# Forgetting attention and a spectral mix: rows 0 to 127 of each weight matrix loaded as row pairs

## The chip, the cores and the metric

The kernel runs on one core of one Trainium2 chip. The metric is the device time of one launch in microseconds. Every run is of the whole kernel, from inputs in the chip's main memory (HBM) to the output there. Engines are called as the profile calls them: PE (TensorE; PEld is its weight load), DVE (VectorE), ACT (ScalarE), POOL (GpSimd), SP (SyncE), and the 16 DMA engines.

## The reference

```python
def _attn_ref(q, k, v, f):                  # q, k, v: (8, 8, 576, 64), f: (8, 8, 576)
    scores = (1.0 / np.sqrt(D)) * np.matmul(q, k.transpose(0, 1, 3, 2))
    cum = np.cumsum(np.log(np.clip(f, 0.0001, 1.0)), axis=-1)
    scores = np.where(causal, -1000000000.0, scores + cum[:, :, :, None] - cum[:, :, None, :])
    attn = softmax(scores)
    return np.matmul(attn, v)

def _moe_ref(x, w_r, w_i, w_ch):            # x: (8, 576, 512), w_r, w_i: (64, 512, 512)
    X = np.fft.rfft(x, axis=1)
    Xr, Xi = np.real(X[:, :64]), np.imag(X[:, :64])
    Yr = np.einsum('bmd,mde->bme', Xr, w_r) - np.einsum('bmd,mde->bme', Xi, w_i)
    Yi = np.einsum('bmd,mde->bme', Xr, w_i) + np.einsum('bmd,mde->bme', Xi, w_r)
    Y[:, :64] = Yr + 1j * Yi
    u = x + np.fft.irfft(Y, n=576, axis=1)
    return u + np.maximum(u @ w_ch, 0.0)
```

Attention over 64 pairs of batch and head gives `x` (8 batches, 576 positions, 512 channels). Along the positions `x` is transformed to 64 frequencies ("modes"). Each mode m has a complex 512 by 512 matrix, `w_r[m] + i w_i[m]`, that is applied to the 8 batches' spectra. The result is transformed back, added to `x`, and goes through one more matrix, `w_ch`. All inputs are float32. The two weight arrays have 64 MiB each and are by far the most of what is read.

## The kernel before, in words

**Attention.** The 64 batch-head pairs are handled two heads at a time: 32 steps, `pairs[i] = (g, b)`, where g (0 to 3) names a group of two heads, 128 channels of `x`, and b is the batch. Group 0 comes first for all eight batches, then group 1, and so on. The loop over `i` has 34 turns; its body is written in a fixed order by hand, and every engine works through its own instructions in that order. In turn `i`, `scores(i, ..)`, `mask` and `back_v` work on step `i`, `trans(i + 1, ..)` and `scale_v(i + 1)` prepare the next, `av` and `norm` finish step `i - 1` and write its part of `x_all` (bf16), and `dft(i - 2)` computes the spectrum of the step before that. POOL's queue issues nearly all loads in program order: in turn `i` q and k of step `i + 4` (five buffers), v of step `i + 3` (four buffers), and one or two halves of a weight tile.

**The spectrum.** `dft` multiplies `x_all[:, g, b, ..]` (positions on the partitions) with the basis `bas3` (blocks sin, cos, -sin of 64 columns each; line 310) into PSUM. For groups 0 and 1 it is five matmuls (one for each block of positions) with all 128 channels as output partitions and 192 columns (line 505). One ACT copy (line 512) puts the result into `XS[:, g]`, ordered mode, block, batch. A slice of 16 columns of one mode then holds (real, imaginary) or (-imaginary, real) for 8 batches, the operand for `w_r` or `w_i`. For groups 2 and 3 the channels are split into even and odd ones, ten matmuls of 64 output partitions (line 521), and copied into `XP` (line 528): partitions 0 to 63 hold pairs of channels of group 2, 64 to 127 those of group 3.

**Weight tiles.** A tile `(u, dc)` belongs to four modes, 4u to 4u + 3, and has 1024 KB in bf16 (the load converts from float32). For `dc` 0 and 1 it holds rows 128·dc to 128·dc + 127 of both `w_r` and `w_i`, one row for each partition, so that each contiguous piece that a DMA reads is one row, 2048 B; the two arrays are two DMAs ("halves", line 156). For `dc` 2 and 3 it holds rows 256 to 511 of one of the two arrays, two neighbouring rows on each partition, so that each piece is 4096 B (line 165). The order of tiles is `wseq`: `(0,0)` to `(15,0)`, `(0,1)` to `(11,1)`, then for each u `(u,1)` if it is not yet there, `(u,2)`, `(u,3)`. There are seven buffers in `wpool`; five of the first tiles are "guests" in space that `x_all` and `yx` need only later.

**Matrix products.** `spec_mms` multiplies one tile, four modes by two parts, eight matmuls with 512 columns (line 194); the four modes go to four groups of 32 output partitions. In attention, from turn 10, `spec_early` does so for the first 28 tiles and adds the results up in `yacc`, that is `yx[:, h, 0:1024]`. After attention, the mode stage goes through u = 0 to 15 with the other tiles, adds `yacc` (line 815), and turns the outcome into `YT`; `xw` and `folds` of the batches are put between. For u = 15 `spec_cols` (line 211) takes the place of `spec_mms`. After the last weight tile the last modes are transformed back and all outputs written, the tail.

Of the kernel before, what the change touches and what calls it, by code (L numbers as in the profile page):

```python
# [10 lines left out]
F32 = mybir.dt.float32  # L11
BF16 = mybir.dt.bfloat16
# [5 lines left out]
def _strided(ap: bass.AP, free_dims, offset_elems: int = 0) -> bass.AP:  # L18
    new_ap = [list(ap.ap[0])] + [list(x) for x in free_dims]
    return bass.AP(tensor=ap.tensor, offset=ap.offset + offset_elems, ap=new_ap)  # L20
# [3 lines left out]
def kernel(  # L24
# [11 lines left out]
    nc = tc.nc  # L36
    B, H, S, Dh = q.shape
    NM = moe_w_r.shape[0]
    D = H * Dh
    assert S == 576 and Dh == 64 and D == 512 and H == 8, (B, H, S, Dh)  # L40
    assert NM == 64 and B == 8
    NSB = 5
    SBLK = [128, 128, 128, 128, 64]
# [9 lines left out]
    XROW = 24 * NM + 32  # L53
# [8 lines left out]
    const = ctx.enter_context(tc.tile_pool(name="const", bufs=1))  # L62
    wpool = ctx.enter_context(tc.tile_pool(name="wpool", bufs=NW))

    yx = const.tile([128, 8, 1280], F32, name="yx")
    x_all = const.tile([128, NEB, B, NSB, 128], BF16, name="x_all")
    XS = const.tile([128, 2, XROW], BF16, name="XS")
    XP = const.tile([128, 2, 24, NM], BF16, name="XP")
    wch = const.tile([128, NEB, D], BF16, name="wch")
    ident_bf = const.tile([128, 128], BF16, name="ident_bf")  # L70
# [5 lines left out]
    bas3 = const.tile([128, NSB, 3, NM], BF16, name="bas3")  # L76
# [21 lines left out]
    psM = actx.enter_context(tc.tile_pool(name="psM", bufs=2, space=PSUM))  # L98
# [28 lines left out]
    for u in range(NU):  # L127
# [4 lines left out]
    guests = {  # L132
        0: x_all[:, 3, :, :, :].rearrange("p b s c -> p (b s c)"),
        2: x_all[:, 2, :, :, :].rearrange("p b s c -> p (b s c)"),
        4: yx[:, 6:8, :].rearrange("p k e -> p (k e)").bitcast(BF16),
        6: yx[:, 4:6, :].rearrange("p k e -> p (k e)").bitcast(BF16),
        11: x_all[:, 3, :, :, :].rearrange("p b s c -> p (b s c)"),
    }

    def issue_w(half=None):  # L140
        n = wissued[0]
        if n >= len(wseq):
            return
        u, dc = wseq[n]
        if half != 1:
            if n in guests:
                w8 = guests[n][:, 0 : 8 * D].rearrange("p (t m e) -> p t m e", t=2, m=4)
            else:
                shape = [128, 2, 4, D] if dc < 2 else [128, 4, 2, D]
                w8 = wpool.tile(shape, BF16, tag="w8", name="w8")  # L150
            wtile[(u, dc)] = w8
        w8 = wtile[(u, dc)]
        if dc < 2:
            for t, src in enumerate((moe_w_r, moe_w_i)):
                if half in (None, t):
                    nc.gpsimd.dma_start(  # L156
                        w8[:, t, :, :],
                        src[4 * u : 4 * u + 4, dc * 128 : (dc + 1) * 128, :].rearrange("m p e -> p m e"),
                    )
        elif half != 1:  # L160
            src = (moe_w_r, moe_w_i)[dc - 2]
            step = 1 if n + 1 == len(wseq) else 4
            for j in range(0, 4, step):
                m = 4 * u + j
                nc.gpsimd.dma_start(  # L165
                    w8[:, j : j + step, :, :].rearrange("p m r e -> p m (r e)"),
                    src[m : m + step, 256:512, :].rearrange("m (p r) e -> p m (r e)", r=2),
                )
        if half != 0:
            wissued[0] += 1  # L170
# [3 lines left out]
    def issue_half():  # L174
        issue_w(whalf[0])
        whalf[0] ^= 1

    XPv = XP[:].rearrange("p r c m -> p (r c) m")

    def spec_mms(A, u, dc, first, last):  # L180
        w8 = wtile.pop((u, dc))
        for n in range(2):
            for j in range(4):
                m = 4 * u + j
                st_, sp_ = first and n == 0, last and n == 1
                if dc < 2:
                    M = 32
                    c0 = m * 24 + (8 if n == 0 else 0)
                    lhsT, rhs = XS[:, dc, c0 : c0 + 32], w8[:, n, j, :]
                else:  # L190
                    M = 32 if st_ else 16
                    c0 = 24 * n + (8 if dc == 2 else 0)
                    lhsT, rhs = XPv[:, c0 : c0 + M, m], w8[:, j, n, :]
                nc.tensor.matmul(  # L194
                    A[32 * j : 32 * j + M, :], lhsT=lhsT, rhs=rhs, start=st_, stop=sp_
                )

    def spec_cols(AT, dc, modes=range(4)):
        u = NU - 1
        w8 = wtile[(u, dc)]  # L200
        for j in modes:
            for eb in range(NEB):
                for n in range(2):
                    m = 4 * u + j
                    if dc < 2:
                        c0 = m * 24 + (8 if n == 0 else 0)
                        lhsT, rhs = w8[:, n, j, eb * 128 : (eb + 1) * 128], XS[:, dc, c0 : c0 + 16]
                    else:
                        c0 = 24 * n + (8 if dc == 2 else 0)
                        lhsT, rhs = w8[:, j, n, eb * 128 : (eb + 1) * 128], XPv[:, c0 : c0 + 16, m]  # L210
                    nc.tensor.matmul(
                        AT[:, eb, 2 * j : 2 * j + 2, :].rearrange("p c b -> p (c b)"),
                        lhsT=lhsT,
                        rhs=rhs,
                        start=(n == 0),
                        stop=(n == 1),
                    )
# [95 lines left out]
        nc.vector.tensor_copy(bas3[:, :, 2, :], Zt[:, :, :, 1])  # L313

    def setup_late():
        nc.vector.memset(XS[:, :, 24 * NM : XROW], 0.0)
        nc.vector.tensor_copy(
            perm[:].rearrange("p (b j ri) -> p b j ri", b=8, j=4),
            ident_bf[:].rearrange("p (j x ri b) -> p b j x ri", j=4, x=2, ri=2)[:, :, :, 0, :],
        )  # L320
        nc.vector.tensor_copy(rep[:], _strided(ident_bf[:, KF:128], [[0, 4], [1, KL]]))
        nc.gpsimd.dma_start(wch[:], moe_w_ch.rearrange("(eb p) e -> p eb e", p=128))
# [175 lines left out]

    def dft(i):
        g, b = pairs[i]  # L500
        if g < 2:
            pd = psM.tile([128, 3, NM], F32, tag="m", name="pd")
            for sc in range(NSB):
                ns = SBLK[sc]
                nc.tensor.matmul(
                    pd[:],
                    lhsT=x_all[:ns, g, b, sc, :],
                    rhs=bas3[:ns, sc, :, :],
                    start=(sc == 0),
                    stop=(sc == NSB - 1),  # L510
                )
            nc.scalar.copy(
                XS[:, g, 0 : 24 * NM].rearrange("p (m c b) -> p c m b", c=3, b=8)[:, :, :, b], pd[:]
            )
            return
        pd = psM.tile([128, 2, 3, NM], F32, tag="m", name="pd2")
        half = slice(64 * (g - 2), 64 * (g - 2) + 64)
        for r in range(2):
            for sc in range(NSB):
                ns = SBLK[sc]  # L520
                nc.tensor.matmul(  # L521
                    pd[half, r, :, :],
                    lhsT=x_all[:ns, g, b, sc, r:128:2],
                    rhs=bas3[:ns, sc, :, :],
                    start=(sc == 0),
                    stop=(sc == NSB - 1),
                )
        nc.scalar.copy(
            XP[half, :, :, :].rearrange("p r (c b) m -> p r c b m", c=3)[:, :, :, b, :], pd[half]
        )  # L530
# [3 lines left out]
    def spec_early(u, dc):  # L534
        if u == NU - 1:
            AT = psM.tile([128, NEB, 8, B], F32, tag="m", name="AT0")
            spec_cols(AT, dc)
            nc.vector.tensor_copy(accT[:], AT[:].rearrange("p e c b -> p e b c"))
            return
        A = psM.tile([128, D], F32, tag="m", name="A0")  # L540
        spec_mms(A, u, dc, True, True)
        if dc == 0:
            nc.scalar.copy(yacc[u // 2][:, u % 2, :], A[:])
        else:
            y = yacc[u // 2][:, u % 2, :]
            nc.vector.tensor_tensor(y, A[:], y, ALU.add)
# [5 lines left out]
    for i in range(NPAIR + 2):  # L552
# [54 lines left out]
        if i >= 2:  # L607
            dft(i - 2)
        if i == 2:
            setup_late()  # L610
# [12 lines left out]
    with ExitStack() as bctx:  # L623
# [44 lines left out]
        with ExitStack() as mctx:  # L668
# [97 lines left out]
            for u in range(NU):  # L766
# [4 lines left out]
                for dc in range(first, NEB):  # L771
# [3 lines left out]
                    if last:  # L775
# [6 lines left out]
                        else:  # L782
# [16 lines left out]
                            for h in range(2):  # L799
                                for to, frm, n in ((YLa[h], 0, 4), (YLw[h], 2, 2), (YLw[h], 0, 2)):  # L800
# [7 lines left out]
                                    )  # L808
                    else:
                        spec_mms(A, u, dc, dc == first, dc == NEB - 1)  # L810
                    issue_w()
                if last:
                    break
# [3 lines left out]
                for eb in range(NEB):  # L817
                    nc.tensor.matmul(
                        yps[:, eb, :],
                        lhsT=Yb[:, eb * 128 : (eb + 1) * 128],  # L820
                        rhs=perm[:],
                        start=True,
                        stop=True,
# [93 lines left out]
        for i in range(len(steps)):  # L917
# [11 lines left out]
            p, sb = steps[i][0]  # L929
# [54 lines left out]
```

## Time and profile before

| | |
|---|---|
| Time, median of 3 runs | 436.8 us (436.75 to 438.17) |
| Profiled execution, its own time | 436.43 us |
| Its span in the profile | 434.6 us |
| Busy: PE, DVE, ACT, POOL | 343.3, 267.9, 234.1, 145.0 us |
| Read from HBM, written to it | 163.7 MB, 9.4 MB |
| DMA packets of POOL's queue (q0) | 62800 |
| Half of a `dc` 0 or 1 tile: issue to landing | 11.1 us (`w_r`), 12.3 us (`w_i`), 27 each, 512 KB |
| A `dc` 2 or 3 tile: issue to landing | 29.5 us (16 of `w_r`), 31.7 us (15 of `w_i`), 1024 KB |

The span is the time from the profile's first to its last instruction; the difference to the execution's own time, 1.8 us, lies around it. Busy time is the time in which an engine executes, not how much of its peak it reaches. The profile counts a DMA's bytes as written, so a float32 load into bf16 moves twice that in reading. Its DMA share adds up the times of all packets over 16 engines; packets overlap, so it can be over 1.

### The profile page before, as it was taken

Reading aid. Unit: us, or ns where it says so; the run is one execution under the profiler, and the core shown is the slowest. Engines: PE = TensorE matmul, PEld = TensorE weight load, DVE = VectorE, ACT = ScalarE, POOL = GpSimd, SP = SyncE. Lnnn points to the kernel's source line nnn. Section 1 sums busy time; section 2 is a strip of 40 time slices with the busy share of each in tenths; the row PEclk is TensorE's granted clock in tenths of the full one; section 3 lists DMA queues with packets and bytes.
Section 4 is the critical chain, followed back from the end, with each engine's and each line's share of the span. In section 5 each row is a group of like instructions: output and inputs, shape, how many; then the busy total and the mean of one; then the engine's idle time right before and its main releaser. Section 6 shows DMA issues by size and latency. Waiting matters only on the chain.

```text
span 434.6 us, 10304 instructions
## 1 busy us (share of the span) xinstructions
PE 343.3 (79%) x4264; PEld 189.6 (44%) x4274; DVE 267.9 (62%) x651; ACT 234.1 (54%) x358; POOL 145.0 (33%) x215
## 2 busy tenths in 40 slices
PE   1689787798898898988896386599877498888993
PEld 1455555554555565555553142244433233334330
DVE  6677888877778778888885122222233165565794
ACT  4556777687887766656660022024322166564783
POOL 6544445444544353444213211111122202110273
PEclk9986999999999999999999579589999699999998
DMA  8999999999999999999999999999999999998498
GB/s 185 205 233 220 233 219 232 225 227 233 231 229 227 226 228 225 228 225 228 227 218 213 212 212 211 212 212 213 211 212 212 209 209 211 210 209 158 168 383 323
DMA packets 68543, 96.76 MB, mean 223 GB/s; under 512 B 3728, under 2 KB 45200, under 8 KB 68496
## 3 DMA queue, kind: packets, MB, share of 16 engines
q0 software_dynamic: 62800, 85.64, 106.3%
q1 hardware_dynamic: 5696, 10.47, 6.6%
q8 instruction: 33, 0.54, 0.4%
q14 instruction: 14, 0.11, 0.1%
HBM read 163.73 MB, written 9.44 MB: 398 GB/s over the span
## 4 chain that ended last, share of the span: by engine, by line
DMA 43%; PE 31%; DVE 18%; issue 3%; ACT 3%; POOL 1%; DVEq 0%; POOLq 0%
DMA w<-in_moe_w_r_dram 22%; DMA w<-in_moe_w_i_dram 20%; PE pav L477 5%; DVE vT L384 4%; DVE qkT L360 4%; DVE x_all L492 4%; PE A L194 4%; PE sps L432 3%; PE tv L382 3%; PE pd L521 3%; PE vp L393 2%; DMA qk<-in_k_dram 2%; PE Z L654 2%; DVE vn L372 2%; PE U L654 2%
## 5 line engine op out<-in xcount | busy, mean ns | idle before, releaser
L439 ACT ACTIVATE et<-sps 128x1024 bf16<-128x1024 f32 x96 | 96.0, 1049 | 13.9 <-PE sps L432 11.5
L477 PE MATMUL pav<-vs,et 128*128 128x65 bf16 (+1 forms) x896 | 52.1, 198 | 0.2 <-DVE vn L372 0.2
L360 DVE COPY qkT<-tp 128x640 bf16<-128x640 bf16 x64 | 48.7, 763 | 2.8 <-PE tp L355 2.8
L815 DVE TENSOR_TENSOR Yb<-A,yx 128x512 bf16<-128x512 f32 x15 | 10.4, 691 | 61.0 <-PE A L194 60.9
L477 PEld LDWEIGHTS <-et 128*128 128x128 bf16 (+1 forms) x896 | 37.2, 103 | 17.9 <-issue 13.6
L432 PE MATMUL sps<-qkT 64*128 64x512 bf16 (+4 forms) x320 | 39.8, 312 | 1.1 <-DVE qkT L360 1.1
L194 PE MATMUL A<-w,XP 128*16 128x512 bf16 (+1 forms) x240 | 21.9, 449 | 23.0 <-DMA w<-in_moe_w_i_dram 12.8
L694 PE MATMUL pxw<-wch,xT 128*128 128x512 bf16 (+1 forms) x152 | 39.0, 402 | 0.9 <-issue 0.3
L492 DVE TENSOR_TENSOR x_all<-pav,rcp 128x384 bf16<-128x384 f32 (+2 forms) x96 | 36.2, 377 | 3.3
L355 PE MATMUL tp<-ident_bf,qk 128*64 128x128 bf16 x576 | 30.3, 237 | 9.3 <-DMA qk<-in_k_dram 9.3
L384 DVE COPY vT<-tv 128x576 bf16<-128x576 bf16 x32 | 24.2, 757 | 19.8 <-PE tv L382 19.8
L165 POOL DMA_DIRECT2D w<-in_moe_w_r_dram x16 | 11.9, 743 | 71.8 <-PE A L194 50.5
L701 ACT CAST XW<-pxw 128x512 bf16<-128x512 f32 (+1 forms) x16 | 9.4, 585 | 47.3 <-PE pxw L694 47.3
L156 POOL DMA_DIRECT2D w<-in_moe_w_r_dram x27 | 20.5, 758 | 38.7 <-DMA w<-in_moe_w_i_dram 9.4
L404 ACT COPY vs<-vp 128x576 bf16<-128x576 bf16 x32 | 20.5, 640 | 21.7 <-PE vp L400 21.7
L165 POOL DMA_DIRECT2D w<-in_moe_w_i_dram x19 | 13.3, 698 | 53.3 <-PE A L194 31.6
L701 ACT CAST yx<-pxw 128x512 bf16<-128x512 f32 (+1 forms) x24 | 14.0, 585 | 31.4 <-PE pxw L694 31.4
L109 POOL DMA_DIRECT2D qk<-in_q_dram x32 | 19.5, 610 | 32.5 <-PE sps L432 6.2
L741 ACT CAST x_all<-pu 128x512 bf16<-128x512 f32 (+1 forms) x40 | 23.4, 584 | 11.2 <-PE pu L740 10.3
L491 DVE RECIPROCAL rcp<-pav 128x6 f32<-128x6 f32 (+2 forms) x96 | 16.2, 169 | 17.4 <-PE pav L477 17.3
L156 POOL DMA_DIRECT2D w<-in_moe_w_i_dram x27 | 20.3, 752 | 18.4 <-DMA w<-in_moe_w_i_dram 8.2
L109 POOL DMA_DIRECT2D qk<-in_k_dram x32 | 19.2, 601 | 19.3 <-DMA w<-in_moe_w_i_dram 5.2
(149 smaller groups left out, 677.8 us busy)
## 6 DMA issues: line engine op xcount, KB each, us to landing
w<-in_moe_w_r_dram POOLq DMA_DIRECT2D x16, 1024.0 KB, 29.5
w<-in_moe_w_i_dram POOLq DMA_DIRECT2D x15, 1024.0 KB, 31.7
w<-in_moe_w_r_dram POOLq DMA_DIRECT2D x27, 512.0 KB, 11.1
w<-in_moe_w_i_dram POOLq DMA_DIRECT2D x27, 512.0 KB, 12.3
out_dram<-o_sb SPq DMA_DIRECT2D x36, 256.0 KB, 3.2
vt<-in_v_dram POOLq DMA_DIRECT2D x29, 288.0 KB, 10.7
qk<-in_q_dram POOLq DMA_DIRECT2D x32, 144.0 KB, 10.8
qk<-in_k_dram POOLq DMA_DIRECT2D x32, 144.0 KB, 10.4
```

What stands on the lines that cost most here:

```text
L109: nc.gpsimd.dma_start(qk[64 * n : 64 * n + 64, :, :], src[b, 2 * g : 2 * g + 2, :, :].rearrange("h (p r) d -> p h (r d)", p=64),)
L156: nc.gpsimd.dma_start(w8[:, t, :, :], src[4 * u : 4 * u + 4, dc * 128 : (dc + 1) * 128, :].rearrange("m p e -> p m e"),)
L165: nc.gpsimd.dma_start(w8[:, j : j + step, :, :].rearrange("p m r e -> p m (r e)"), src[m : m + step, 256:512, :].rearrange("m (p r) e -> p ...
L194: nc.tensor.matmul(A[32 * j : 32 * j + M, :], lhsT=lhsT, rhs=rhs, start=st_, stop=sp_)
L355: nc.tensor.transpose(tp[64 * hp : 64 * hp + 64, r - r0, :, :].rearrange("p n c -> p (n c)"), qk[:, hp, r * 64 : r * 64 + 64], ident_bf[:, :],
L360: nc.vector.tensor_copy(st[i]["T"][:].rearrange("p n (c r) -> p n c r", r=9)[:, :, :, r0:r1], tp[:, 0 : r1 - r0, :, :].rearrange("p r n c ...
L384: nc.vector.tensor_copy(st[i]["vT"][:].rearrange("p (c r) -> p c r", r=9), tv[:].rearrange("p r c -> p c r"))
L432: nc.tensor.matmul(ps[:, hp, c : c + n], lhsT=KT[sl, jb * 128 : jb * 128 + 128], rhs=QT[sl, i0 : i0 + n], start=True, stop=True,)
L439: nc.scalar.activation(st[i]["et"][:, T, :, :], ps[:], ACT.Exp, scale=scale)
L477: nc.tensor.matmul(pav[:Ms, sb % 3, hp, :], lhsT=eblk(i, hp, jb, sb), rhs=rhs, start=(jb == 0), stop=(jb == sb),)
L492: nc.vector.tensor_tensor(x_all[:ns, g, b, lo:hi, :].rearrange("p s (h d) -> p s h d", h=2), pav[:ns, lo % 3 : lo % 3 + n, :, 0:Dh], _stri ...
L694: nc.tensor.matmul(pxw[rows, :], lhsT=xT[:, eb, sb * 128 : sb * 128 + Ms], rhs=wch[:, eb, :], start=(eb == 0), stop=(eb == NEB - 1),)
```

## The change

Tiles `(u, 0)`, rows 0 to 127, get another layout. The 128 rows of `w_r` become 64 pairs of neighbouring rows, 4096 B each, on partitions 0 to 63; the 128 rows of `w_i` become 64 pairs on partitions 64 to 127. A tile keeps its size and its two DMAs, which now write 64 partitions each. The spectrum of group 0 must match: partitions 0 to 63 need channel pairs as `w_r` multiplies them, partitions 64 to 127 the same pairs as `w_i` does. `dft` for g = 0 therefore makes twenty matmuls of 64 output partitions and 128 columns (even and odd channels, five blocks of positions, two halves of partitions), and two ACT copies into a new place, `x0`, which lies in `yx[:, h, 1024:1280]` for h = 2, 3, 5, 7. `XS` keeps group 1 alone. The two matmuls of a mode in `spec_mms` are now the even and the odd rows rather than `w_r` and `w_i`.

```diff
-    XS = const.tile([128, 2, XROW], BF16, name="XS")
+    XS = const.tile([128, XROW], BF16, name="XS")
...
-                    nc.gpsimd.dma_start(
-                        w8[:, t, :, :],
-                        src[4 * u : 4 * u + 4, dc * 128 : (dc + 1) * 128, :].rearrange("m p e -> p m e"),
-                    )
+                    rows = src[4 * u : 4 * u + 4, dc * 128 : (dc + 1) * 128, :]
+                    if dc == 0:
+                        nc.gpsimd.dma_start(
+                            w8[64 * t : 64 * t + 64, :, :, :].rearrange("p m r e -> p m (r e)"),
+                            rows.rearrange("m (p r) e -> p m (r e)", r=2),
+                        )
+                    else:
+                        nc.gpsimd.dma_start(w8[:, t, :, :], rows.rearrange("m p e -> p m e"))
...
+    def x0(h):
+
+        return yx[:, h, 2 * D : 1280].bitcast(BF16).rearrange("p h (c m) -> p h c m", m=16)
+
+    def xri(c0, n, m):
+
+        h = (2, 3, 5, 7)[m // 16]
+        return x0(slice(h, h + 1))[:, 0, c0 : c0 + n, m % 16]
...
-                if dc < 2:
-                    M = 32
+                M = 32 if st_ or dc == 1 else 16
+                if dc == 0:
+                    lhsT, rhs = xri(16 * n, M, m), w8[:, j, n, :]
+                elif dc == 1:
                     c0 = m * 24 + (8 if n == 0 else 0)
-                    lhsT, rhs = XS[:, dc, c0 : c0 + 32], w8[:, n, j, :]
+                    lhsT, rhs = XS[:, c0 : c0 + 32], w8[:, n, j, :]
...
-        nc.vector.memset(XS[:, :, 24 * NM : XROW], 0.0)
+        nc.vector.memset(XS[:, 24 * NM : XROW], 0.0)
...
-        if g < 2:
+        if g == 0:
+            pd = psM.tile([128, 4, NM], F32, tag="m", name="pd")
+            for r in range(2):
+                for sc in range(NSB):
+                    ns = SBLK[sc]
+                    for t in range(2):
+                        nc.tensor.matmul(
+                            pd[64 * t : 64 * t + 64, 2 * r : 2 * r + 2, :],
+                            lhsT=x_all[:ns, g, b, sc, r:128:2],
+                            rhs=bas3[:ns, sc, 1 - t : 3 - t, :],
+                            start=(sc == 0),
+                            stop=(sc == NSB - 1),
+                        )
+            for n, h in enumerate((slice(2, 4), slice(5, 8, 2))):
+                nc.scalar.copy(
+                    x0(h).rearrange("p h (x b) m -> p h x b m", b=8)[:, :, :, b, :],
+                    pd[:].rearrange("p x (h m) -> p h x m", m=16)[:, 2 * n : 2 * n + 2, :, :],
+                )
+            return
+        if g == 1:
```

The same two cases are made in `spec_cols`, and the shapes of the tiles and the copy into `XS` follow.

More of the change, by code (lines that the diff above doesn't have):

```diff
@@ L146, in issue_w @@
             if n in guests:
-                w8 = guests[n][:, 0 : 8 * D].rearrange("p (t m e) -> p t m e", t=2, m=4)
+                w8 = guests[n][:, 0 : 8 * D].rearrange("p (m r e) -> p m r e", m=4, r=2)
             else:
-                shape = [128, 2, 4, D] if dc < 2 else [128, 4, 2, D]
+                shape = [128, 2, 4, D] if dc == 1 else [128, 4, 2, D]
                 w8 = wpool.tile(shape, BF16, tag="w8", name="w8")
@@ L185, in spec_mms @@
                 st_, sp_ = first and n == 0, last and n == 1
-                if dc < 2:
-                    M = 32
+                M = 32 if st_ or dc == 1 else 16
+                if dc == 0:
+                    lhsT, rhs = xri(16 * n, M, m), w8[:, j, n, :]
+                elif dc == 1:
                     c0 = m * 24 + (8 if n == 0 else 0)
-                    lhsT, rhs = XS[:, dc, c0 : c0 + 32], w8[:, n, j, :]
+                    lhsT, rhs = XS[:, c0 : c0 + 32], w8[:, n, j, :]
                 else:
-                    M = 32 if st_ else 16
                     c0 = 24 * n + (8 if dc == 2 else 0)
@@ L204, in spec_cols @@
                     m = 4 * u + j
-                    if dc < 2:
+                    if dc == 0:
+                        lhsT, rhs = w8[:, j, n, eb * 128 : (eb + 1) * 128], xri(16 * n, 16, m)
+                    elif dc == 1:
                         c0 = m * 24 + (8 if n == 0 else 0)
-                        lhsT, rhs = w8[:, n, j, eb * 128 : (eb + 1) * 128], XS[:, dc, c0 : c0 + 16]
+                        lhsT, rhs = w8[:, n, j, eb * 128 : (eb + 1) * 128], XS[:, c0 : c0 + 16]
                     else:
@@ L512, in dft @@
             nc.scalar.copy(
-                XS[:, g, 0 : 24 * NM].rearrange("p (m c b) -> p c m b", c=3, b=8)[:, :, :, b], pd[:]
+                XS[:, 0 : 24 * NM].rearrange("p (m c b) -> p c m b", c=3, b=8)[:, :, :, b], pd[:]
             )
```

## The prediction

> **What bounds the kernel now.** I read the page's slices first, then its chain, then windows with a DMA column, then PE's timeline reduced to rows that a DMA released.
>
> ```profile
> span 434.6 us, 10304 instructions
> ...
> PE   1689787798898898988896386599877498888993
> ...
> DMA  8999999999999999999999999999999999998498
> ...
> DMA 43%; PE 31%; DVE 18%; issue 3%; ACT 3%; POOL 1%; DVEq 0%; POOLq 0%
> ```
>
> The DMA line is full from the second slice to about 400 us, through attention (to about 232 us) and the mode stage alike, while PE leaves gaps. The chain gives DMA 43%, all but a little of it weight loads after 202 us. The chain does not show that attention is DMA-fed as well; POOL's issues do. With each issue the trace keeps its landing: from 8 to 211 us nearly every issue follows the landing of the DMA eight places before it by 0.28 to 0.57 us. So eight DMAs are always outstanding, about 11 us of work (page, issue to landing: 11.1 and 12.3 us for weight halves). After 217 us POOL waits for weight buffers instead (`POOL w L165 <- PE A L194: 82.1`), but with six or seven 1024 KB loads under way (29.5 us to landing). The stream never runs dry; its total work sets when the last weights land, 402.12 us. Then comes a 32.5 us tail without weights.
>
> Windows price the two row lengths (columns: PE, PEld, DVE, ACT, POOL busy, PE clock, DMA share, GB/s written):
>
> ```profile
> 280.00:300.00 20.00, 17.97 (x122) 8.32 (x124) 6.05 (x13) 5.85 (x10) 2.96 (x4) 0.87 1.12 212
> 356.00:357.50 1.50, 1.50 (x7) 0.38 (x5) 1.50 (x3) 1.14 (x3) 0.00 (x0) 1.00 1.22 203
> 371.00:372.50 1.50, 0.68 (x12) 0.17 (x7) 0.27 (x1) 0.00 (x0) 0.14 (x1) 1.00 1.22 207
> ```
>
> 280:300 moves only 4096 B rows; the short windows move nearly only 2048 B rows (of `(u,1)`). Bytes written are half of those read. 212 against some 206 (with the 209 of 341 to 342.5) is the difference that the change is about.
>
> ```profile
> 272.61 1.07 PE L194 MATMUL A<-w,XP 128*16 128x512 bf16 x8 [3.96 <-DMA w<-in_moe_w_i_dram]
> 277.55 1.11 PE L194 MATMUL A<-w,XP 128*32 128x512 bf16 x8 [2.69 <-DMA w<-in_moe_w_r_dram]
> 341.88 1.06 PE L194 MATMUL A<-w,XP 128*16 128x512 bf16 x8 [4.25 <-DMA w<-in_moe_w_i_dram]
> 397.15 1.08 PE L211 MATMUL AT<-XP,w 128*128 128x16 bf16 x32 [0.49 <-DMA w<-in_moe_w_r_dram]
> 402.16 0.40 PE L211 MATMUL AT<-XP,w 128*128 128x16 bf16 x8 [0.31 <-DMA w<-in_moe_w_i_dram]
> ```
>
> PE waits for weights several times, 4.25 us at 341.88; near the end the waits are short because PE is then nearly full, but it restarts from each landing.
>
> **The transfer.** The 16 tiles `(u,0)` go from two halves of 512 packets (2048 B read, 1024 written) to two of 256 (4096 and 2048): 8192 packets fewer. Price of one tile's 1024 KB: by landings, 21 loads of 4096 B rows between 237.86 and 341.84 us make 4.95 us each; four pairs of 2048 B halves late in the stream landed 5.08 to 5.14 us after the load before them, 5.12 on average. Difference 0.17 us, times 16: 2.75 us. By rates, 1048576 B at 206 and at 212 GB/s are 5.09 and 4.95 us: 2.3 us. By packet times, 98 ns at a DMA share of 1.215 is 80.7 ns of an engine, 173 ns at 1.116 is 155.0; 161.4 less 155.0, times 32 packets per engine and tile, is 0.20 us, 3.3 us in all. I take 2.75, bounds 2.3 and 3.3.
>
> All 16 tiles land by 135 us, inside the full stretch. POOL issues sooner by what is gained, eight stay outstanding, and later loads move up. At 217 us some 15 us of transfers are queued (to 233.13); buffers freed no sooner leave 13. PE's waits of 3.96 and 4.25 us exceed 2.75, so its work moves up with the landings, and so does the tail.
>
> **Half the partitions.** Each new DMA writes only 64 partitions. The nearest row is q and k, also 64 partitions: 144 KB halves land 0.744 us apart (mean of 26), 198 GB/s, with 1152 B packets of 107 ns, just what their length asks for between 98 and 173 ns. Their rows are short and each DMA has an end, so 198 is a lower bound; the 4096 B rows' 212 is the upper one. Summing a late attention cycle (two weight halves 5.12, v 0.70, q and k, 7.35 together) leaves 1.53 us for q and k, 0.76 each, much of it the smaller packet. I take 212, because packet length decides every other row.
>
> [...] The q and k rows agree that nothing halves; no run here shows a long transfer of this kind.
>
> **The spectrum.** In eight iterations (`i` from 2 to 9) `dft` changes: five matmuls of 128 columns by 192 become twenty of 64 by 128.
>
> ```profile
> L512 ACT CAST XS<-pd 128x192 bf16<-128x192 f32 x5 | 5.2, 1041 | 1.8 <-PE pd L505 1.8
> 50.76 0.31 PEld L355 LDWEIGHTS <-qk 128*64 128x64 bf16 x10
> 50.77 0.47 PE L355 MATMUL tp<-ident_bf,qk 128*64 128x128 bf16 x10
> 214.27 1.25 PE L521 MATMUL pd<-bas,x_all 128*64 128x192 bf16 x9
> 54.25 0.69 PE L505 MATMUL pd<-bas,x_all 128*128 128x192 bf16 x5
> ```
>
> Ten of L355, which alternate halves of the output as the new ones do, take 0.47 us: twenty 0.94, plus 0.25 over 0.69. Serial, like L521 (nine in 1.25), they would take 2.8, plus 2.1. I take 0.25, as the form is L355's. (The rows: one group of the window 40 to 70 us, busy total and mean ns behind the bar; then the timeline, start and duration of merged runs.) Behind them on PE stand the next iteration's scores. ACT gives back: one strided copy of 1.04 us becomes two of 128 elements in runs of 16; between 0.22 (64 elements, L426) and 0.47 (384, L528) that is some 0.55 together. In eight iterations PE gains 2 us of work (bound 17) and ACT loses 4.
>
> Cover: the DMA queue. POOL loads q some 24 us before DVE copies its transposes; five buffers at 6.35 us allow 31.7. So compute may lag 7.7 us before an issue waits, and 11 more before the queue empties. The guest tile at 90.45 us needs the slot that `(0,0)` leaves (matmuls at 86.00): 3.8 us plus 11. Only the 17 us bound would open a gap, of about 2 us. The copies now write into `yx`, columns 1024 to 1279 of rows 2, 3, 5 and 7, where no weight guest and no `yacc` lies, so I count no wait; were rows 5 to 7 held as one block, ACT's copy at 35.8 us would wait for the guest in rows 6 and 7, landing at 42.79 and 49.45: 13.7 us once at most, under the same cover. After attention PE's waits of 3.8, 2.7, 4.0 and 2.7 us from 242 to 278 take up a lag.
>
> The early `spec_mms` keep eight matmuls (0.61 us for XS, the same for `XP`'s wider stride); smaller memset and fewer descriptors: nothing.
>
> **Sum.** 436.43 (span 434.6 plus 1.8 around it) less 2.75 is 433.7. The median of the runs, 436.8, lies 0.37 higher: 434.0.
>
> **Rivals.** [...] (2) *Slower by the same mechanism*: at q and k's 198 GB/s a tile takes 5.29 us, 0.17 over today's 5.12, 16 times 2.75: 439.5. It decides from where such a load falls under 205 GB/s (1048576 B in 5.12 us). For it: those are the only 64-partition rows. Against: their short packets explain most of it. (3) *PE takes over at the end*: if its work did not move up, only the waits of 0.3 to 0.5 us could shrink: 436.4. Against: the 4.25 us wait ahead. (4) *The loads split into 1024 B writes still*: 436.8. Against: `(u,2)`, with the same source pattern, writes 2048 B packets.
>
> **Numbers.** Half a percent, 2.2 us, is about what a measurement of this kernel tells from no change. Forecast 0.54; rival 1 0.18, rivals 3 and 4 0.08 together, rival 2 0.20. The forecast's bound of 2.3 lies at the threshold, so a little of it goes to same: faster 0.51, same 0.29, slower 0.20. The range goes from 433.0 (3.3 gained, and a few tenths of scatter) to 439.5.
>
> **What would show it.** Right: 16384 packets of 1024 B gone and 8192 of 2048 B come; the same share of DMA to 400 us; last weights at about 399.4; `dft` near 0.94 us and its ACT copies under 0.6; the tail still 32.5 us. Wrong: new halves landing 2.6 us apart or more in a run of their own; packets of the new size over 173 ns; POOL's issues in attention behind PE or ACT rather than the eighth DMA before; PE without waits before 397 us.

## The result, and the profile after

The change makes the kernel slower: median 443.75 us of 6 runs (443.21 to 450.91) against 437.12 us of 6 runs (436.29 to 438.17) before. The ratio is 1.0158, 95% interval 1.0129 to 1.0187, so some 6.9 us. The forecast was a gain, to 434.0, in a range from 433.0 to 439.5. Ratios here leave disturbed runs out and medians don't, so the two need not agree, least of all in e3_half_2048, where two of four runs were disturbed and the other two took 442.86 and 443.75 us. The profiled execution after took 446.10 us (span 444.3), 2.4 over its median; differences from profiles are therefore read at landings of loads, not at the end.

First the rows of the page before that the prediction does not show, then the page after:

```profile
GB/s 185 205 233 220 233 219 232 225 227 233 231 229 227 226 228 225 228 225 228 227 218 213 212 212 211 212 212 213 211 212 212 209 209 211 210 209 158 168 383 323
DMA packets 68543, 96.76 MB, mean 223 GB/s; under 512 B 3728, under 2 KB 45200, under 8 KB 68496
```

```profile
span 444.3 us, 10566 instructions
...
PE   1688888889789888788894397599877599888993
...
DMA  8999999999999999999999999999999999995498
GB/s 191 209 237 216 211 201 213 221 222 222 218 211 228 221 231 221 231 218 225 228 218 212 212 213 212 211 212 212 212 212 211 209 210 210 211 209 98 158 370 326
DMA packets 60352, 96.78 MB, mean 218 GB/s; under 512 B 3728, under 2 KB 28816, under 8 KB 60304
```

The packets are what the change says: 68543 became 60352, 8191 fewer. DMA is as full as before, to about 405 us. But the GB/s row is lower in slices 4 to 12, where the changed tiles are loaded, although the pieces are longer: 201 to 222, where the kernel before has 219 to 233. The DMA row, 9 in these slices of both, shows that the engines are held, not what they move.

Windows make it plain (columns as in the prediction; the last two are DMA share and GB/s written). The kernel before:

```profile
10.00:35.00 25.00, 18.78 (x239) 12.91 (x240) 17.66 (x45) 13.52 (x23) 11.71 (x18) 0.88 1.22 217
40.00:130.00 90.00, 75.42 (x1330) 49.27 (x1325) 72.48 (x202) 69.65 (x95) 41.80 (x65) 1.00 1.21 228
260.00:340.00 80.00, 60.30 (x432) 27.98 (x437) 21.72 (x44) 20.47 (x35) 13.33 (x18) 0.91 1.12 212
```

and after:

```profile
10.00:35.00 25.00, 19.77 (x254) 13.28 (x254) 18.13 (x46) 13.52 (x23) 11.09 (x18) 1.00 1.15 220
40.00:130.00 90.00, 77.17 (x1421) 51.46 (x1420) 71.58 (x199) 65.75 (x100) 35.33 (x59) 1.00 1.15 214
260.00:340.00 80.00, 64.87 (x454) 29.30 (x453) 21.72 (x44) 22.19 (x38) 13.33 (x18) 0.90 1.12 212
```

From 10 to 35 us the change gains what its longer pieces promise, 220 against 217. From 40 to 130 us it loses, 214 against 228. After attention the rate is the same. The early window has two v loads from POOL, the middle one a v load in every turn. The packets say which loads suffer (their mean time, from the trace): a v packet, 4608 B read and 4608 written, took 184 ns from 35 to 60 us before and 271 after, and 187 and 289 from 60 to 90 us; 61 and 75% of them were over 1.2 times their usual time. Of the new tiles' packets only 11% were, and the usual one took 173 ns as in the mode stage; but they are many, and on average they took 180 to 184 ns. Added up from 35 to 130 us, the time beyond the usual is 4.5 us per DMA engine in v's packets, 3.3 in the new tiles' and 0.7 in q's and k's. From 10 to 35 us no kind of packet is stretched, though two v loads are among them (184 ns).

What follows is moved as a whole. PE's restarts by landing loads, after:

```profile
279.33 1.06 PE L208 MATMUL A<-w,XP 128*16 128x512 bf16 x8 [3.61 <-DMA w<-in_moe_w_i_dram]
284.26 1.11 PE L208 MATMUL A<-w,XP 128*32 128x512 bf16 x8 [2.69 <-DMA w<-in_moe_w_r_dram]
348.61 1.07 PE L208 MATMUL A<-w,XP 128*16 128x512 bf16 x8 [3.81 <-DMA w<-in_moe_w_i_dram]
404.86 1.09 PE L227 MATMUL AT<-XP,w 128*128 128x16 bf16 x32 [1.67 <-DMA w<-in_moe_w_r_dram]
```

Against 272.61, 277.55 and 341.88 before, each is 6.7 us late; `(15,2)`, the last row, 7.7. The chain of the page after has a new member to match, `DMA vt<-in_v_dram 13%`, which the chain before did not list among its largest.

This execution's tail is 2.4 us longer than the one before, 34.9 us against 32.5, with a PE clock of 0.83 from 400 to 420 us, where it was 1.00; that is as much as the execution lies over its median.

### The profile page after: what moved, and what is told of

It reads as the page before. It is cut to its first block, busy times and chain, and to the rows that moved or that the text cites. A ratio compares the mean times of both kernels' runs of the same rounds, so it can differ in the third digit from the quotient of the medians.

```text
span 444.3 us, 10566 instructions
## 1 busy us (share of the span) xinstructions
PE 351.4 (79%) x4394; PEld 193.4 (44%) x4394; DVE 268.3 (60%) x651; ACT 230.7 (52%) x366; POOL 140.6 (32%) x215
## 2 busy tenths in 40 slices
DMA packets 60352, 96.78 MB, mean 218 GB/s; under 512 B 3728, under 2 KB 28816, under 8 KB 60304
## 4 chain that ended last, share of the span: by engine, by line
DMA 47%; PE 32%; DVE 13%; issue 4%; ACT 2%; POOL 1%; DVEq 0%; POOLq 0%; ACTq 0%
DMA w<-in_moe_w_i_dram 18%; DMA w<-in_moe_w_r_dram 14%; DMA vt<-in_v_dram 13%; PE A L208 4%; PE pxw L729 4%; DVE vT L400 3%; PE pav L493 3%; DVE qkT L376 3%; DVE x_all L508 2%; PE sps L448 2%; PE U L689 2%; PE Z L689 2%; DMA qk<-in_k_dram 2%; PE tv L398 2%; DVE vn L388 2%
## 5 line engine op out<-in xcount | busy, mean ns | idle before, releaser
L455 ACT ACTIVATE et<-sps 128x1024 bf16<-128x1024 f32 x96 | 93.8, 1026 | 18.5 <-PE sps L448 17.0
L729 PE MATMUL pxw<-wch,xT 128*128 128x512 bf16 (+1 forms) x160 | 40.6, 409 | 0.0
L169 POOL DMA_DIRECT2D w<-in_moe_w_r_dram x16 | 11.9, 741 | 71.2 <-PE A L208 48.3
L169 POOL DMA_DIRECT2D w<-in_moe_w_i_dram x19 | 13.3, 698 | 53.3 <-PE A L208 36.6
L388 DVE TENSOR_TENSOR vn<-vt,wn 128x576 bf16<-128x576 f32 x32 | 24.0, 749 | 9.8 <-DMA vt<-in_v_dram 7.9
L371 PEld LDWEIGHTS <-qk 128*64 128x64 bf16 x576 | 19.4, 116 | 12.7 <-issue 8.2
```

Source lines behind the costliest of these rows:

```text
L169: nc.gpsimd.dma_start(w8[:, j : j + step, :, :].rearrange("p m r e -> p m (r e)"), src[m : m + step, 256:512, :].rearrange("m (p r) e -> p ...
L371: nc.tensor.transpose(tp[64 * hp : 64 * hp + 64, r - r0, :, :].rearrange("p n c -> p (n c)"), qk[:, hp, r * 64 : r * 64 + 64], ident_bf[:, :],
L388: nc.vector.tensor_tensor(vn[:], st[i]["vt"][:], _strided(wn[:, widx(i), :], [[1, 9], [0, Dh]]), ALU.mult)
L455: nc.scalar.activation(st[i]["et"][:, T, :, :], ps[:], ACT.Exp, scale=scale)
L729: nc.tensor.matmul(pxw[rows, :], lhsT=xT[:, eb, sb * 128 : sb * 128 + Ms], rhs=wch[:, eb, :], start=(eb == 0), stop=(eb == NEB - 1),)
```

## The experiments

In the table, `(15,2)` is the landing of that tile in the profiled execution, the load before the last four; GB/s is that of the window 40 to 130 us.

| Kernel | Median us | Ratio to before (95%) | `(15,2)` | GB/s |
|---|---|---|---|---|
| before | 436.8 to 437.1 | 1 | 397.11 | 228 |
| after | 443.75 | 1.0158 (1.0129 to 1.0187) | 404.81 | 214 |
| e1_pairs_128 | 436.28 | 0.9996 (0.9978 to 1.0014) | 395.21 | 232 |
| e2_spectrum | 437.21 | 1.0003 (0.9987 to 1.0020) | 397.56 | 228 |
| e5_alternate | 436.01 | 0.9985 (0.9967 to 1.0002) | 395.27 | 232 |
| e3_half_2048 | 446.79 | 1.0142 (1.0118 to 1.0166) | 403.52 | 217 |
| e4_v_bf16_after | 436.35 | 0.9987 (0.9975 to 0.9999) | 397.00 | 208 (v counts half) |
| e4_v_bf16_before | 439.59 | 1.0056 (1.0039 to 1.0074) | 400.20 | 206 (v counts half) |
| e7_late_halves | 438.08 | 1.0021 (1.0005 to 1.0038) | | 228 |
| e6_alternate_matched | 437.76 | 1.0004 (0.9982 to 1.0026) | 399.35 | 221 |
| e8_v_bf16_sp | 436.10 | 0.9979 (0.9963 to 0.9996) | 397.35 | 208 (v counts half) |
| e9_straddle | 437.21 | 1.0008 (0.9980 to 1.0035) | 397.72 | 228 |
| e10_alternate_3 | 439.16 | 1.0042 (1.0012 to 1.0073) | 397.83 | 228 |

**The pieces, without the half.** The changed kernel, `(u,0)` loaded as row pairs onto all partitions:

```diff
-                            w8[64 * t : 64 * t + 64, :, :, :].rearrange("p m r e -> p m (r e)"),
-                            rows.rearrange("m (p r) e -> p m (r e)", r=2),
+                            w8[:, 2 * t : 2 * t + 2, :, :].rearrange("p m r e -> p m (r e)"),
+                            src[m0 : m0 + 2, 0:256, :].rearrange("m (p r) e -> p m (r e)", r=2),
```

(with `m0 = 4 * u + 2 * t`.) Theory A of this and the next runs, a guess to be tested: a DMA that writes 64 neighbouring partitions loses rate, above all beside v. For this run it has the loss gone, some 434 us, with v packets back at about 184 ns.

> The changed kernel, but each half of a (u,0) tile is loaded onto all 128 partitions: rows 0 to 255 of two modes as 128 row pairs, so the same 512 KB in the same 256 packets of 4096 B read. It leaves the right weights out (the tile holds other rows), everything else is as in the changed kernel. [...] Theory B (the longer transform of group 0 delays compute, and with it the issue of loads): unchanged, 443.7. Theory C (pieces of 4096 B among the short ones of attention are the harm): unchanged, 443.7. Theory D (64 partitions in a DMA, whichever they are): 434.

```profile
40.00:130.00 90.00, 77.49 (x1424) 51.79 (x1425) 72.16 (x201) 65.83 (x101) 41.50 (x66) 1.00 1.14 232
```

(The window of this run.) Measured: 436.28, v packets back at 182 to 187 ns. So it is neither the longer piece (C) nor the spectrum (B). The gain is smaller than A's 434, of which more below.

**The spectrum alone.**

```diff
-                            w8[64 * t : 64 * t + 64, :, :, :].rearrange("p m r e -> p m (r e)"),
-                            rows.rearrange("m (p r) e -> p m (r e)", r=2),
+                            w8.rearrange("p m r e -> p (m r) e")[:, 4 * t : 4 * t + 4, :],
+                            rows.rearrange("m p e -> p m e"),
```

> The spectrum of the change alone: twenty matmuls, two copies, operands from the new place, but the loads of before (128 rows of 2048 B onto 128 partitions). It leaves out the match of rows and spectrum. Theory A: 437, as before the change, within 1 us. Theory B: 443 to 444. Theories C and D: 437.

Measured: 437.21, ratio 1.0003. Theory B falls: the longer `dft` costs nothing that these runs can tell, at most 0.2%. In its profile `(15,2)` lands 0.45 us later than before.

**The same DMAs on other partitions.** The source, the 64 partitions for each DMA, the 256 packets stay; only which partitions changes:

```diff
-                            w8[64 * t : 64 * t + 64, :, :, :].rearrange("p m r e -> p m (r e)"),
+                            w8[t:128:2, :, :, :].rearrange("p m r e -> p m (r e)"),
```

> The changed kernel, but w_r goes to the even and w_i to the odd partitions: the same two DMAs, the same 64 partitions in each, the same 256 packets of 4096 B, only spread over all 128 instead of a contiguous half. The spectrum stays in halves, so the products mix rows. [...] Theories B, C and D: 443 to 444.

```profile
10.00:35.00 25.00, 18.86 (x246) 12.95 (x246) 18.05 (x45) 13.51 (x23) 10.94 (x18) 0.88 1.15 220
40.00:130.00 90.00, 78.20 (x1383) 52.26 (x1382) 70.39 (x193) 64.17 (x98) 39.27 (x65) 0.95 1.14 232
```

(Windows of this run.) 436.01 us, where A had 434 to 435: the whole loss is gone with the place alone, 232 GB/s where the change had 214, v packets at 181 ns. Theory D falls too, and any explanation by the order of reading from HBM, since the reading is the same. Against the change as it is, `(15,2)` lands 9.5 us sooner in the profiled executions; the medians are 7.7 us apart.

**Halves with the old pieces.** The tile in the order parity, mode, so that two neighbouring rows do not join:

```diff
-                            w8[64 * t : 64 * t + 64, :, :, :].rearrange("p m r e -> p m (r e)"),
-                            rows.rearrange("m (p r) e -> p m (r e)", r=2),
+                            w8[64 * t : 64 * t + 64, :, :, :],
+                            rows.rearrange("m (p r) e -> p r m e", r=2),
```

> The changed kernel with its halves of the partitions, but each row as a piece of its own: the tile is ordered parity, mode, so that 512 packets of 2048 B are written into 64 partitions. All of the computation is kept. Theory A: the loss stays, without the longer packets' gain: 442 to 447. Theory B: 443 to 444, plus up to 2.7 for the shorter packets. Theory C: 437. Theory D: 442 to 447.

```profile
40.00:130.00 90.00, 78.28 (x1404) 52.05 (x1400) 72.24 (x199) 64.80 (x99) 38.13 (x61) 0.98 1.22 217
```

Slower by 1.42%, 217 GB/s, v packets at 243 to 276 ns. The loss comes with halves of the partitions and short pieces too.

**Is v needed for it?** Two more theories stood then. A1: weights into half the partitions lose by themselves. A2: they lose only beside v, the one load that is written unconverted. Two tests. First v converted as it is loaded, in the changed kernel and in the one before:

```diff
-        vt = vpool.tile([128, 9, Dh], F32, tag="vt", name="vt")
+        vt = vpool.tile([128, 9, Dh], BF16, tag="vt", name="vt")
...
-    for i in range(3):
-        load_v(i, nc.sync)
     load_qk(0)
+    load_v(0)
```

> The changed kernel with v converted to bf16 as it is loaded (all v loads from POOL, the first three too), so that a v packet writes 2304 B for 4608 B read instead of 4608. Everything is computed. To be read against the next run. [...] Theory A1 (the half-partition weights lose by themselves, v is only a bystander): 6 to 9 us over the next run.

> The kernel of before with the same v loads in bf16, the base for the run above. Both theories: 436 to 440, the reading being the same and v's few loads at the start moving behind q and k.

Measured: 436.35 and 439.59. With v at half the bytes written, the changed kernel is the faster one, by 3.2 us, and `(15,2)` lands 3.2 us sooner (397.00 against 400.20). Windows of the changed kernel with it, then of its base:

```profile
40.00:130.00 90.00, 77.62 (x1432) 51.84 (x1428) 72.21 (x200) 66.22 (x102) 38.96 (x66) 1.00 1.16 208
```

```profile
40.00:130.00 90.00, 74.86 (x1311) 48.91 (x1311) 72.88 (x201) 69.10 (x95) 40.22 (x63) 1.00 1.23 206
```

208 over 206: the change's gain, about as first forecast. A2 was expected to end within 2 us of the base and went beyond it; A1's 6 to 9 us over is excluded. In both traces a v load is 128 packets of 1152 B written, instead of 64 of 4608, and not packets of 2304 B as the expectation says. So v's bytes and the length of its packets changed together, and these runs do not tell which of the two the harm needs. The base itself is 2.5 us slower than the kernel before. It has three more v loads from POOL and twice as many packets for each; what each of these costs was not tested.

Second, half-partition loads where there is no v:

```diff
-                nc.gpsimd.dma_start(
-                    w8[:, j : j + step, :, :].rearrange("p m r e -> p m (r e)"),
-                    src[m : m + step, 256:512, :].rearrange("m (p r) e -> p m (r e)", r=2),
-                )
+                for hf in range(2):
+                    nc.gpsimd.dma_start(
+                        w8[64 * hf : 64 * hf + 64, j : j + step, :, :].rearrange("p m r e -> p m (r e)"),
+                        src[m : m + step, 256 + 128 * hf : 384 + 128 * hf, :].rearrange(
+                            "m (p r) e -> p m (r e)", r=2
+                        ),
+                    )
```

> The kernel of before with its last 31 tiles (rows 256 to 511, row pairs, after attention, when no v, q or k is loaded) each loaded by two DMAs of 64 partitions (row pairs 0 to 63, then 64 to 127) instead of one of 128. Same packets, same tile, everything computed. Theory A1: 31 tiles at the 0.4 to 0.6 us that a tile lost in the changed kernel, 449 to 456. [...]

```profile
260.00:340.00 80.00, 64.73 (x445) 28.96 (x444) 21.75 (x44) 21.05 (x36) 19.87 (x32) 0.87 1.12 211
```

438.08, about 1.0 us over the kernel before for 32 tiles in halves (the edit takes in the last tile too, which is loaded mode by mode); 211 GB/s for 212 in the window. A1 would have had 12 us or more, A2 437 to 438. Twice as many DMAs are in it, so even of that 1.0 not all need be the halves' own. (Its profiled execution was 4.5 us over its median, so only the rate is read from it.)

**Which partitions lose.** Back in the changed kernel, w_r across partition 64, w_i in two DMAs on its two sides:

```diff
+                        for p0, p1, st, q0 in (((32, 96, 1, 0),), ((0, 32, 1, 0), (96, 128, 1, 32)))[t]:
+                            nq = (p1 - p0 + st - 1) // st
+                            nc.gpsimd.dma_start(
+                                w8[p0:p1:st, :, :, :].rearrange("p m r e -> p m (r e)"),
+                                rows[:, 2 * q0 : 2 * q0 + 2 * nq, :].rearrange("m (p r) e -> p m (r e)", r=2),
+                            )
```

> The changed kernel, but w_r goes to partitions 32 to 95 in one DMA and w_i to 0 to 31 and 96 to 127 in two; the products mix rows, since the spectrum stays in halves. It asks whether the harm hangs on neighbouring partitions or on the split at partition 64. [...] If neighbouring partitions as such are the harm: 443 to 445.

The same loop with `((0, 128, 2, 0),), ((1, 64, 2, 0), (65, 128, 2, 32))`:

> The same three DMAs for a tile, on alternate partitions: w_r on the even ones, w_i on the odd ones from 1 to 63 and from 65 to 127 (again only the w_i ones stay on one side of partition 64). It shows what a third DMA among eight outstanding costs, and whether spreading within one side helps. [...] If only neighbours crowd: 436 to 437.

```profile
40.00:130.00 90.00, 77.61 (x1416) 52.05 (x1414) 72.56 (x200) 65.13 (x100) 43.85 (x76) 1.00 1.14 228
```

```profile
40.00:130.00 90.00, 77.06 (x1407) 51.41 (x1404) 72.73 (x203) 65.56 (x101) 43.46 (x76) 1.00 1.14 228
```

In the window both move 228 GB/s, between 214 and 232, and `(15,2)` lands at 397.72 and 397.83, 2.5 us after e5_alternate's 395.27: a quarter of the change's 9.5. Of the v packets from 35 to 130 us, 5 to 15% were stretched, against 42 to 75% in the change. So 64 neighbouring partitions do little harm when they lie on both sides of partition 64, and w_i's 32 partitions to a DMA, which stay on one side, cost as much alternate as neighbouring. That fits a split at 64 and not the neighbourhood. A split elsewhere was not tried, and whatever the third DMA of a tile costs is within the 2.5 us. The medians, 437.21 (under the 443 to 445 of harm by neighbouring partitions) and 439.16 (over the 436 to 437 of harm by neighbours alone), differ more than the streams do; the runs of the second scatter from 435.29 to 441.67, and I draw nothing from that difference.

**Versions to keep.** Alternate partitions with a spectrum to match need a permutation of partitions, since the matmuls of `dft` leave halves: one ACT copy to SBUF, one matmul with a permuted identity, then the two copies.

```diff
+        nc.tensor.matmul(px[:], lhsT=alt[:], rhs=st[i]["xe"][:], start=True, stop=True)
```

> A version of the change that computes everything: w_r on the even and w_i on the odd partitions, and a matmul with a permutation puts the spectrum of group 0 there (in each of eight turns one more matmul of 256 columns and one more ACT copy). Theories A1 and A2: as the alternating run before, 435.5 to 436.5, under the kernel of before by 0.4 to 1.3. If compute decided after all: 438 or more.

437.76, runs from 434.71 to 441.59: a miss. POOL's timeline in its profile shows why (start, duration, operation, idle time before and its releaser):

```profile
87.86 0.60 POOL L110 DMA_DIRECT2D qk<-in_k_dram  x1 [0.58 <-DMA w<-in_moe_w_i_dram]
96.66 0.64 POOL L159 DMA_DIRECT2D x_all<-in_moe_w_r_dram  x1 [8.20 <-PE A L209]
```

Two rows of its page:

```profile
PEclk9999987589999999999999979589989699899998
GB/s 188 208 236 222 236 223 233 234 165 221 224 236 235 219 234 219 234 219 233 228 217 206 196 212 211 213 211 214 210 212 211 209 210 212 208 210 183 161 384 323
```

Compute is behind, and the guest tile waits 8.2 us for the slot that `(0,0)` leaves; the GB/s falls to 165 in that slice, the ninth. It is the one place where the prediction's cover was thin, and here it ran out. In the slice before, from 76 to 87 us, the PE clock is down to 0.5 of full speed; whether the added work alone would have used up the cover is not shown.

The other version keeps halves and converts v, but leaves the first three v loads on SP in float32:

> The changed kernel with v in bf16 from the fourth load on (POOL), and the first three v loads as before the change, float32 from SP. Everything is computed. Theory A2 (unconverted v beside half-partition weights is the loss): the last weights land 2 to 3 us earlier than in the kernel of before, and the time is 434 to 435, under both kernels. If v in bf16 only bought its gain by the other order of the first loads: 436 to 437 or more. Theory A1 (halves lose by themselves): 441 or more.

436.10 us, 0.9979 (0.9963 to 0.9996): faster than the kernel before, by 0.2%, less than the 434 to 435 expected. In its profiled execution (2.3 us over the median, with a tail of 34.8 us) the stream is ahead of the kernel before by 1.0 us at the landing of `(14,2)` (381.07 for 382.12), instead of 2 to 3; at `(15,2)` it is level with it. v has twice as many packets here (128 for 64 a load), which may eat a part of the change's gain; this was not tested by itself.

## Why the prediction was wrong

**What bounds the kernel: right.** The time followed the DMA stream. After the change the landings were 6.7 us late from 140 us on, PE's restarts were late by the same, and the median moved by 6.6.

**The transfer: right in kind, its size open.** 2.75 us were forecast, bounds 2.3 and 3.3. Where the loss is gone, the stream gains 2.3 us by `(15,2)` (397.56 with the spectrum alone, to 395.21 and 395.27 with pairs spread out), and 3.2 where v is converted, there by the medians as well. But in the first comparison the medians show only 0.9 to 1.2 us, less than the lower bound. The landings are of one execution each, that with the spectrum alone 0.8 us over its median and the other two 1.1 and 0.5 under, so they overstate the difference. I can't settle the size more closely than between 0.9 and 3.2 us.

**Half the partitions: the step that failed.** I took 212 GB/s for the new loads, the rate of 4096 B rows on all partitions, because packet length decided every other row, and had 198 below it, from q and k, which are themselves loads to half the partitions. For such loads by themselves 212 was good: they pass at 211 in e7_late_halves, and most of the new packets took 173 ns. In the stream of attention it was not. From 35 to 140 us a weight half landed 2.73 us after the load before it on average, 192 GB/s, for 2.55 in e5_alternate, and a v load 1.19 us after it, for 0.77. What the step left out is the neighbour in the queue. v's rows were in the same views: before the change it usually writes 288 KB in 0.70 to 0.74 us by the landings (median of 15 loads 0.74), some 400 to 420 GB/s, twice the 212 of a weight load. The loss against e5_alternate, 9.5 us by the landings, comes to 0.7 us for each of 14 v loads from POOL between 35 and 140 us. My reading is that a tile to one half and a float32 v load beside it delay each other; what delays them is not shown, only which partitions, and which v, take the loss away (e5_alternate, 232 GB/s in the window; e4_v_bf16_after, 3.2 us under its base). One row does not fit this reading as it stands: the two v loads from POOL before 35 us land between new halves as well and were not stretched (184 ns), though in e3_half_2048 the same two were (246 ns).

**The split at partition 64.** The runs agree with a split at partition 64: a tile with one load across it lands `(15,2)` 2.5 us late, a quarter of the 9.5 of a tile on single sides, even with the other load still on single sides. Why one side loses is not shown. The 212 GB/s that I took for a half leave v out: with no v loaded 211 pass (e7_late_halves), beside v in float32 192 by the landings.

**Rivals.** Rival 2, slower because a load writes only half the partitions, was the right side and place at a chance of 0.20, but its price came from q and k, 2.75 us of loss. The loss was 6.9, and its threshold "under 205 GB/s" is met in attention, at 192, and not where no v is loaded, at 211. Rival 1, at 0.18, is a gain partly eaten by a small loss on each load; no run shows a loss of the size it took: e7_late_halves has 1.0 us over 32 tiles, 0.03 each, and the change lost 6.9 in all. Rival 4 falls by the packet count, rival 3 by the restarts that moved as one.

**The spectrum: right in its effect.** 0.94 us were forecast for twenty matmuls, 1.18 us measured from first to last, so that they add 0.5 us and not 0.25; 0.55 for the two copies, 0.54 measured (269 ns each). The effect on the time is within 0.2%. The cover held: in the change 61 of POOL's 70 issues from 35 to 140 us still follow the landing of the eighth DMA before them by 0.2 to 0.65 us, as 65 of 75 did before, and in e6_alternate_matched the guest slot was the first thing to run dry.

**What would show it.** Of the signs listed, "packets of the new size over 173 ns" came true on average (180 to 184 ns from 35 to 130 us) and not for the usual packet. The larger stretch was v's, which no sign named.

## What to carry to other kernels

When a load is narrowed to part of the partitions, list what all loads in flight write to that part before calling a rate that fits one load alone safe: here 211 GB/s passed with no v loaded, and 192 by the landings beside v. Beside v, loads to 64 partitions were cheaper when spread over both sides of partition 64 (232 GB/s in the window on alternate partitions, 228 with one of two loads across 64, 214 in halves). A DMA share that stays at its level says nothing about bytes (1.15 at 214 GB/s, 1.14 at 232): compare GB/s in equal windows. A neighbour's packets can be where the time goes (here 4.5 us per DMA engine in v's, 3.3 in the new tiles'), so look at every load in the window, not only at the changed one.

## What the runs showed of the hardware that I had not expected

- Tiles to 64 partitions passed at 211 GB/s where no v is loaded (e7_late_halves, 260 to 340 us). Beside v in float32 to 128 partitions (some 400 to 420 GB/s by its usual landings before) both were stretched in the change from 35 us on: v packets from 184 and 187 to 271 and 289 ns, the new tiles' from 173 to between 180 and 184 on average; the window's rate was 214 GB/s, where it is 232 with the same pieces on all partitions (e1_pairs_128).
- A DMA whose destination steps over every second partition (e5_alternate) cost no more than one on all partitions (e1_pairs_128): 232 GB/s in the window for both.
- One v load was 64 packets of 4608 B written in float32, and 128 packets of 1152 B written where it is converted on the way (e4_v_bf16_after, e4_v_bf16_before).
